# Normalising the first group's softmax on two engines, and re-ordering its hand-over to the MLP

## The chip, the cores and the metric

One NeuronCore of a Trainium2 chip runs the whole program. The metric is device time in microseconds (us) of one execution. Single executions of one kernel scatter by some tenths of a microsecond (before: 295.57 to 295.91 in three runs).

Engines: PE is TensorE's matmul, DVE is VectorE, ACT is ScalarE, POOL is GpSimd, SP issues the DMA transfers. An engine "stands" while it is idle; a "hole" is such a stand between two groups of its instructions.

## The reference, cut to what matters

```python
def _attn_ref(q, k, v):                      # q, k, v: (8, 8, 576, 64)
    k_p = k.reshape(B, H, Sp, 8, D).mean(axis=3)         # pooled by 8: Sp = 72
    v_p = v.reshape(B, H, Sp, 8, D).mean(axis=3)
    scores = scale * np.matmul(q, k_p.transpose(0, 1, 3, 2))
    attn = np.exp(scores - max); attn = attn / (attn.sum(-1) + 1e-9)
    return np.matmul(attn, v_p)

def _moe_ref(x, w_in, w_out):                # x: (4608, 512)
    h = x @ w_in                             # 512 -> 2048
    g = gelu_tanh(h)
    return g @ w_out                         # 2048 -> 512
```

## The kernel before

The 4608 rows are worked in nine groups: one for the first 512 rows of each batch and one for the left-over rows. While TensorE does the MLP of one group, the attention of the next is slipped in between its products, at numbered places called hooks. Group 0 has no predecessor, so its attention runs with nothing to hide behind, in four blocks of 128 rows (j = 0 to 3). Its MLP starts as soon as blocks 0 and 1 are done.

```python
def cast_q(g, j0, j1, eng):        # q from fp32 to bf16, two of the four blocks
    copy(eng, st[g]["qb"][:, j0:j1], st[g]["q"][:, :, j0:j1].rearrange(...))

def norm(g, j, eng):               # one block of the softmax, 8 heads x 72
    nc.vector.reduce_sum(out=den, in_=e, axis=AX.X)
    nc.vector.reciprocal(out=r, in_=den)
    eng.tensor_tensor(out=o, in0=e, in1=r (broadcast), op=ALU.mult)
# ... (cut)
    # front of group 0
    norm(0, 0, nc.vector)
    norm(0, 1, nc.vector)
    e_transpose_pe(0, 0, nc.scalar, "mm")
    q_transpose_pe(0, 2, nc.scalar, "mm")
    q_transpose_pe(0, 3, nc.scalar, "mm")
    warm_up(2, "sc")
    e_transpose_pe(0, 1, nc.vector, "mm")
    for j in (2, 3):
        scores(0, j)
    exps(0, 2)
    for x in range(2):
        values_half(0, 0, x, [nc.vector, nc.scalar][x], "mm")
    exps(0, 3)
# ... (cut)
    # group 1 inside the MLP of group 0; the number is the MLP product ahead of which it is issued
    at(hooks, 72, pool, 1, 0, 4)                     # VectorE, needs k of group 1
    at(hooks, 72, dup_k, 1, 0, 4)
    at(hooks, 72, pool, 1, 4, 5)
    at(hooks, 72, dup_k, 1, 4, 5)
    at(hooks, 80, cast_q, 1, 0, 2, nc.gpsimd)        # needs q of group 1
    at(hooks, 80, cast_q, 1, 2, 4, nc.vector)
    at(hooks, 108, k_transpose_pe, 1, 0, 5)
    at(hooks, 108, k_spread, 1, [nc.vector, nc.vector])
    for j in range(4):
        at(hooks, [114, 118, 122, 125][j], q_transpose_pe, 1, j, nc.vector, "sc")
# ... (cut)
    tail_of_attention(hooks, 1, 188)                 # value products of group 1
```

The softmax here doesn't subtract the row's maximum and nothing guards it: scores larger than these inputs give would overflow.

## Time and profile before

| before | value |
|---|---|
| time, median of 3 runs | 295.87 us |
| span of the profiled run | 293.9 us |
| first MLP product of group 0 | 17.84 us |
| first GELU | 19.98 us |
| last k transpose / first q transpose of group 1 | 32.51 / 33.83 us |
| first scores of group 1 | 36.26 us |
| first MLP product of group 1 | 52.38 us |

A line of a timeline reads: start, time from the first to the last instruction of the line, engine, source line, operation, output<-inputs, shapes, number of instructions, and in brackets how long the engine had been idle and what ended that. A line of the chain reads: start, length, and what the kernel's end was waiting for in that time. The views themselves are shown in the prediction. The waits view adds what an engine waited for in sum: ScalarE and VectorE have long waits everywhere; those that PE does not end up waiting for cost nothing, as PE is busy 97% of the span.

### The profile page before, as it was taken

To read this page: it belongs to the slowest core of one execution; us is meant where nothing else is said; L and a number is where in the kernel's file an instruction comes from. 1 tells how busy PE (TensorE), PEld (TensorE's weight loads), DVE (VectorE), ACT (ScalarE), POOL (GpSimd) and SP (SyncE) were. 2 spreads that over 40 slices of the span, in tenths; PEclk is the share of its full clock that TensorE was granted. 3 is DMA by queue.
4 is the path that set the end of the run, shared out by engine and by line. 5 is a ranking of instruction groups with operands and counts; after the bars stand their busy time and mean duration, and the time that the engine had idled before them with its cause. 6 is when DMAs were issued, how large, how long until landed. Compare 5 with 4: busy or idle time off the path is not lost.

```text
span 293.9 us, 4585 instructions
## 1 busy us (share of the span) xinstructions
PE 286.0 (97%) x1741; PEld 142.7 (49%) x1741; DVE 141.1 (48%) x233; ACT 155.4 (53%) x228; POOL 65.1 (22%) x88
## 2 busy tenths in 40 slices
PE   7889999999999999999999999999999999999996
PEld 3568854445444544454445444544444544444444
DVE  5883769075617570747065806481739100920012
ACT  1475584768067716671576257724673367427500
POOL 3594433221402040114002400240024000100000
PEclk9999999999999999999999999999999999999999
DMA  7999998995599369945994599059944900351012
GB/s 242 357 386 348 382 369 191 342 254 166 129 294 280 116 134 270 265 147 132 263 284 149 126 256 299 7 114 248 285 145 103 170 35 2 81 115 38 0 71 71
DMA packets 73301, 56.32 MB, mean 192 GB/s; under 512 B 45888, under 2 KB 55488, under 8 KB 73280
## 3 DMA queue, kind: packets, MB, share of 16 engines
q1 hardware_dynamic: 73136, 55.98, 70.2%
q8 instruction: 13, 0.21, 0.3%
q10 hardware_dynamic: 144, 0.07, 0.1%
q14 instruction: 8, 0.07, 0.1%
HBM read 36.70 MB, written 9.44 MB: 157 GB/s over the span
## 4 chain that ended last, share of the span: by engine, by line
PE 87%; DMA 7%; SPq 3%; ACT 1%; POOL 1%; issue 0%; DVE 0%; POOLq 0%
PE mm L341 41%; PE mm L325 38%; DMA q_sb<-in_q_dram 5%; DMA w_in_s<-in_moe_w_in_dram 3%; PE xo L291 3%; PE sc L214 2%; PE mm L369 1%; SPq L94 1%; SPq L99 1%; SPq L418 1%; ACT xT L79 1%; PE xo L300 1%; POOL q_b L81 1%; PE mm L336 1%; SPq L92 0%; SPq L111 0%
## 5 line engine op out<-in xcount | busy, mean ns | idle before, releaser
L341 PE MATMUL mm<-w_out_b,gT 128*128 128x512 bf16 x560 | 128.8, 379 | 0.0
L325 PE MATMUL mm<-xT,w_in_b 128*128 128x512 bf16 x512 | 112.0, 379 | 0.3 <-ACT xT L79 0.3
L327 ACT ACTIVATE gT<-mm 128x512 bf16<-128x512 f32 x128 | 76.3, 597 | 38.6 <-PE mm L325 38.6
L341 PEld LDWEIGHTS <-gT 128*128 128x128 bf16 x560 | 52.8, 98 | 59.7 <-issue 2.9
L325 PEld LDWEIGHTS <-w_in_b 128*128 128x128 bf16 x512 | 50.1, 98 | 61.0 <-issue 0.8
L81 DVE COPY osb<-mm 128x512 f32<-128x512 f32 (+2 forms) x37 | 24.2, 658 | 57.6 <-PE mm L341 55.3
L79 ACT CAST xT<-xo 128x1024 bf16<-128x1024 f32 (+1 forms) x18 | 16.6, 967 | 56.9 <-PE xo L291 48.2
L154 POOL TENSOR_TENSOR vbd<-kvb,vmask 128x256 bf16<-128x256 bf16 (+2 forms) x40 | 21.2, 553 | 105.9 <-DVE kvb L134 105.7
L236 DVE TENSOR_REDUCE den<-e 128x8 f32<-128x576 f32 x36 | 26.5, 737 | 36.8 <-ACT e L229 36.8
L132 DVE TENSOR_TENSOR kv<-kv 128x1024 f32<-128x1024 f32 (+3 forms) x19 | 21.9, 1154 | 38.2 <-DMA kv<-in_v_dram 33.3
L229 ACT ACTIVATE e<-sc 128x576 f32<-128x576 f32 x36 | 22.5, 649 | 10.2 <-ACT e L229 5.9
L241 DVE TENSOR_TENSOR eb<-e,r 128x576 bf16<-128x576 f32 x26 | 26.0, 998 | 0.9
L81 POOL CAST q_b<-q_sb 128x2048 bf16<-128x2048 f32 (+2 forms) x9 | 17.6, 1950 | 13.9 <-DMA q_sb<-in_q_dram 13.9
L241 POOL TENSOR_TENSOR eb<-e,r 128x576 bf16<-128x576 f32 x6 | 6.9, 1148 | 58.7 <-ACT e L229 31.4
L336 PE MATMUL mm<-xT,w_in_b 128*128 128x256 bf16 x128 | 15.6, 272 | 0.3 <-DVE xT L81 0.3
L214 PEld LDWEIGHTS <-qT 128*128 128x128 bf16 x128 | 9.9, 98 | 7.3 <-issue 0.8
L214 PE MATMUL sc<-kbd,qT 128*128 128x144 bf16 x128 | 13.1, 226 | 0.4 <-ACT qT L79 0.2
L336 PEld LDWEIGHTS <-w_in_b 128*128 128x128 bf16 x128 | 12.2, 98 | 1.9 <-issue 0.5
L338 ACT ACTIVATE gT<-mm 128x512 bf16<-128x512 f32 x16 | 9.4, 597 | 6.5 <-PE mm L336 6.5
L133 DVE TENSOR_TENSOR kv<-kv 128x512 f32<-128x512 f32 (+3 forms) x19 | 12.4, 651 | 0.6
L536 ACT ACT_TABLE_LOAD x8 | 10.3, 1283 | 0.1
L81 POOL CAST w_in_b<-w_in_s 128x512 bf16<-128x512 f32 (+1 forms) x12 | 9.1, 796 | 1.5 <-DMA w_in_s<-in_moe_w_in_dram 1.5
(58 smaller groups left out, 117.9 us busy)
## 6 DMA issues: line engine op xcount, KB each, us to landing
out_dram<-osb SPq DMA_DIRECT2D x31, 256.0 KB, 6.8
kv<-in_k_dram SPq DMA_DIRECT2D x7, 1024.0 KB, 7.3
q_sb<-in_q_dram SPq DMA_DIRECT2D x7, 1024.0 KB, 5.9
kv<-in_v_dram SPq DMA_DIRECT2D x6, 1024.0 KB, 8.9
w_in_s<-in_moe_w_in_dram SPq DMA_DIRECT2D x8, 512.0 KB, 9.1
w_out_s<-in_moe_w_out_dram SPq DMA_DIRECT2D x4, 1024.0 KB, 13.8
kv<-in_v_dram SPq DMA_DIRECT2D x4, 512.0 KB, 10.1
out_dram<-osb SPq DMA_DIRECT2D x9, 128.0 KB, 2.3
```

The costliest lines, as they stand in the source:

```text
L79: eng.copy(out=out, in_=in_)
L81: eng.tensor_copy(out=out, in_=in_)
L132: add(out=t[:, :, 0:4, :], in0=t[:, :, 0:4, :], in1=t[:, :, 4:8, :], op=ALU.add)
L154: eng.tensor_tensor(out=vbd[p0:128, b, n0:n1, :].rearrange("p (c r) (hh d) -> p c (r hh) d", c=max(m, 1), d=D), in0=kvb[p0:128, 4 + c0:4 + ...
L214: nc.tensor.matmul(out=o, lhsT=qT[:, j, pr, :], rhs=kbd[:, g, pr].rearrange("d hh s -> d (hh s)"), start=True, stop=True)
L229: nc.scalar.activation(out=e.rearrange("p (x h) s -> p x (h s)", x=2), in_=sc[:, :, 0:4 * Sp], func=ACT.Exp, scale=1.0 / 64.0)
L236: nc.vector.reduce_sum(out=den, in_=e, axis=AX.X)
L241: eng.tensor_tensor(out=o.rearrange("p (h s) -> p h s", s=Sp), in0=e, in1=r.unsqueeze(2).to_broadcast([128, H, Sp]), op=ALU.mult)
L325: nc.tensor.matmul(out=hp, lhsT=w_in_b[:, ko, fo * 128:(fo + 1) * 128], rhs=st[g]["xT"][:, ko, :], start=(i == 0), stop=(i == KO - 1))
L327: nc.scalar.activation(out=gT[:, fo, :], in_=hp, func=ACT.Gelu_apprx_tanh)
L336: nc.tensor.matmul(out=hp[:, f, :], lhsT=w_in_b[:, ko, (fo + f) * 128:(fo + f + 1) * 128], rhs=st[g]["xT"][:, ko, c0:c0 + 256], start=(ko ...
L341: nc.tensor.matmul(out=o, lhsT=gT[:, fo, r * 128:(r + 1) * 128], rhs=w_out_b[:, fo, :], start=(fo == 0), stop=(fo == FO - 1))
```

## The change

The intent is to start group 0's MLP sooner. Blocks 0 and 1 are multiplied by the reciprocal of their sums on VectorE (5 heads) and ScalarE (3 heads, one instruction each) side by side; the first value products go ahead of the last scores; two warm-up products go; half of the first w_in chunk is cast on VectorE. The copy of block 2's transposed q moves from ScalarE to VectorE. Further down, the two halves of group 1's q cast change engines, the hooks of its four q transposes move one product later, and that of its value products one earlier.

```diff
--- before.py
+++ after.py
@@ -230,10 +230,17 @@
                              func=ACT.Exp, scale=1.0 / 64.0)
         st[g][("e", j)] = e
 
-    def norm(g, j, eng):
+    def sums(g, j):
         e = st[g][("e", j)]
         den = work.tile([128, H], F32, name="den")
         nc.vector.reduce_sum(out=den, in_=e, axis=AX.X)
+        st[g][("den", j)] = den
+
+    def norm(g, j, eng):
+        e = st[g][("e", j)]
+        if ("den", j) not in st[g]:
+            sums(g, j)
+        den = st[g].pop(("den", j))
         r = work.tile([128, H], F32, name="r")
         nc.vector.reciprocal(out=r, in_=den)
         o = eb[:, j, 128 * 5 - W:]
@@ -245,6 +252,18 @@
                               in0=e.rearrange("p (hh pr) s -> p hh pr s", hh=2),
                               in1=r.rearrange("p (hh pr) -> p hh pr", hh=2).unsqueeze(3).to_broadcast([128, 2, HP, Sp]),
                               op=ALU.mult)
+
+    def norm_two(g, j, h0):
+
+        e = st[g][("e", j)]
+        sums(g, j)
+        r = work.tile([128, H], F32, name="r")
+        nc.vector.reciprocal(out=r, in_=st[g].pop(("den", j)))
+        o = eb[:, j, 128 * 5 - W:].rearrange("p (h s) -> p h s", s=Sp)
+        nc.vector.tensor_tensor(out=o[:, 0:h0], in0=e[:, 0:h0], in1=r[:, 0:h0].unsqueeze(2).to_broadcast([128, h0, Sp]),
+                                op=ALU.mult)
+        for h in range(h0, H):
+            nc.scalar.activation(out=o[:, h], in_=e[:, h], func=ACT.Copy, scale=r[:, h:h + 1])
 
     def eT_tile(g):
         st[g]["eT"] = work.tile([128, 4, 5, 128], BF16, name="eT", bufs=1)
@@ -478,28 +497,30 @@
         scores(0, j)
         exps(0, j)
     pool(0, 5, 7)
+    norm_two(0, 0, 5)
     spread_v(0, nc.gpsimd, (0,))
     pool_pe(0, 7, 9, 1, nc.scalar)
     spread_v(0, nc.gpsimd, (1,))
     cast_q(0, 2, 4, nc.gpsimd)
     spread_v(0, nc.gpsimd, (2,))
-    norm(0, 0, nc.vector)
-    norm(0, 1, nc.vector)
+    norm_two(0, 1, 5)
     e_transpose_pe(0, 0, nc.scalar, "mm")
-    q_transpose_pe(0, 2, nc.scalar, "mm")
+    q_transpose_pe(0, 2, nc.vector, "mm")
     q_transpose_pe(0, 3, nc.scalar, "mm")
-    warm_up(2, "sc")
     e_transpose_pe(0, 1, nc.vector, "mm")
-    for j in (2, 3):
-        scores(0, j)
+    cast_w_in(0, 2, nc.vector)
+    scores(0, 2)
     exps(0, 2)
     for x in range(2):
         values_half(0, 0, x, [nc.vector, nc.scalar][x], "mm")
+    scores(0, 3)
+    sums(0, 2)
     exps(0, 3)
     nc.scalar.preload_act_table_set(GELU_SET)
     norm(0, 2, nc.vector)
     norm(0, 3, nc.vector)
-    for c in range(4):
+    cast_w_in(0, 0, nc.gpsimd)
+    for c in range(1, 4):
         cast_w_in(c, 0, nc.gpsimd)
         cast_w_in(c, 2, nc.gpsimd, 0, 256)
         cast_w_in(c, 2, nc.gpsimd, 256, 512)
@@ -548,14 +569,14 @@
     at(hooks, 72, dup_k, 1, 0, 4)
     at(hooks, 72, pool, 1, 4, 5)
     at(hooks, 72, dup_k, 1, 4, 5)
-    at(hooks, 80, cast_q, 1, 0, 2, nc.gpsimd)
-    at(hooks, 80, cast_q, 1, 2, 4, nc.vector)
+    at(hooks, 80, cast_q, 1, 0, 2, nc.vector)
+    at(hooks, 80, cast_q, 1, 2, 4, nc.gpsimd)
     at(hooks, 108, kT_tile, 1, "sc")
     at(hooks, 108, qT_tile, 1)
     at(hooks, 108, k_transpose_pe, 1, 0, 5)
     at(hooks, 108, k_spread, 1, [nc.vector, nc.vector])
     for j in range(4):
-        at(hooks, [114, 118, 122, 125][j], q_transpose_pe, 1, j, nc.vector, "sc")
+        at(hooks, [115, 119, 123, 126][j], q_transpose_pe, 1, j, nc.vector, "sc")
     at(hooks, 110, cast_w_out, 0, 1, nc.gpsimd)
     at(hooks, 110, cast_w_out, 1, 2, nc.gpsimd)
     at(hooks, 110, cast_w_out, 2, 4, nc.gpsimd)
@@ -575,7 +596,7 @@
     at(hooks, 156, q_tile, 2)
     at(hooks, 156, load_q, 2, 0, 4, nc.sync)
     at(hooks, 156, load_kv, 2)
-    tail_of_attention(hooks, 1, 188)
+    tail_of_attention(hooks, 1, 187)
     mlp_first(0, hooks)
 
     for n_, g in enumerate(seq):
```

## The prediction

> **What bounds the kernel now.** I read the page first: engine shares, then the chain that ended last.
>
> ```profile
> PE 286.0 (97%) x1741; PEld 142.7 (49%) x1741; DVE 141.1 (48%) x233; ACT 155.4 (53%) x228; POOL 65.1 (22%) x88
> ...
> PE 87%; DMA 7%; SPq 3%; ACT 1%; POOL 1%; issue 0%; DVE 0%; POOLq 0%
> ```
>
> TensorE is busy 97% of the 293.9 us span and holds 87% of the chain. Whatever is to be won lies in the 13% that is not PE, and the change touches only the first group, so I asked where that 13% sits: the chain in order of time (start, length, what).
>
> ```profile
> 7.42 8.31 DMA w_in_s<-in_moe_w_in_dram
> 15.75 2.37 SPq L94
> 18.80 13.24 DMA q_sb<-in_q_dram
> 32.19 1.59 POOL q_b L81
> 37.57 2.37 PE mm L341 x11
> 40.20 0.86 PE mm L341 x4
> ```
>
> This is the view that decides the prediction. Until 33.8 us the chain does not run through the softmax of group 0 at all. It runs through the loads: the weights, the issue of group 1's k, group 1's q (landing at about 32 us), then a 1.59 us cast of it on GpSimd. Only then is TensorE the bound. The windows view agrees: DMA share 1.05 to 1.08 in every 10 us stretch from 10 to 40 us, so those landings move with bandwidth and not with the computation.
>
> Then the PE timeline (start, busy, instructions, idle before and its releaser).
>
> ```profile
> 15.43 0.45 PE L255 MATMUL tp<-identb,eb 128*128 128x128 bf16 x5
> 15.72 0.66 PE L214 MATMUL sc<-kbd,qT 128*128 128x144 bf16 x8
> 16.46 1.03 PE L270 MATMUL xo<-eT,vbd 128*128 128x256 bf16 x8
> 17.84 2.02 PE L336 MATMUL mm<-xT,w_in_b 128*128 128x256 bf16 x16 [0.35 <-DVE xT L81]
> ...
> 32.20 0.52 PE L180 MATMUL kT<-identb,kvb 128*128 128x128 bf16 x5
> 32.65 0.83 PE L336 MATMUL mm<-xT,w_in_b 128*128 128x256 bf16 x6
> 33.83 0.40 PE L199 MATMUL tp<-identb,q_b 128*128 128x128 bf16 x4 [0.35 <-POOL q_b L81]
> ```
>
> The first MLP product starts at 17.84. At 32.20 PE transposes group 1's k, and at 33.83 its q, after a hole.
>
> The VectorE timeline shows what the k transposes need.
>
> ```profile
> 28.47 1.23 DVE L132 TENSOR_TENSOR kv<-kv 128x1024 f32<-128x1024 f32 x1 [4.11 <-DMA kv<-in_k_dram]
> ...
> 32.09 0.18 DVE L147 COPY kvb<-kvb 128x64 bf16<-128x64 bf16 x1
> 32.18 0.69 DVE L81 CAST q_b<-q_sb 128x1024 bf16<-128x1024 f32 x1
> ```
>
> Pooling starts the moment k lands (28.47) and its last piece is ready at 32.27, so TensorE arrives at the k transposes with almost no slack.
>
> **What the Trainium skill says.** (1) "SBUF — State Buffer", Who interferes with whom: VectorE and GpSimd share a port pair, taken as an exclusive lock by VectorE casts in a 2-port mode, and contended by two-input VectorE operations. The trace agrees: when both casts of q start at 32.18, VectorE's takes its 0.69 us and GpSimd's 1.58 (1.12 for the same shape at 13.06); a 128x576 multiply takes 0.76 us at 40.08 with GpSimd mostly idle, but 1.01 to 1.15 in the first 22 us. (2) "VectorE: DVE Perf Modes", The TRN2 errata: an fp32 two-input operation takes (N+151)/0.96 ns. For 576 that is 757 ns; the trace has 757. For 360 it gives 532 ns. (3) "ScalarE: Activation LUTs", What ACT_TABLE_LOAD costs: 186 + 0.833 N ns, 93 more for a per-partition operand, 93 of overlap back to back. For N=576 that is 666; the trace has 649. For 72 with a scale operand it gives an estimate of 339 ns, so three take 339 + 2x246 = 0.83 us; no instruction of this form is in the trace before.
>
> **The change, part by part.**
>
> Normalising on two engines. Block 0's multiply now ends near 13.1 (before 13.29), but PE is busy with the v pooling products until 13.34: nothing gained. Block 1: its sum starts about 0.2 earlier, its reciprocal is done near 13.97, VectorE's 5 heads need 0.53 plus a short wait for GpSimd's cast of q, so about 14.65; ScalarE's three end near 14.85. Before, block 1 was ready at 15.37: 0.5 us gained. The price: six ScalarE instructions (2 x 0.83 = 1.7 us), which push the copy of the first transposed block from 13.83-14.52 to about 14.8-15.5.
>
> Transposes and warm-up. Two removed dummy products were 0.43 us in a wait. The second block's transposes go from 15.43 to about 14.9, their VectorE copy from 15.92-16.41 to about 15.4-15.9, so the value products start near 15.95 instead of 16.46. Moving the last scores behind them saves PE nothing in itself: the eight scores (0.66) already fitted into the wait for that copy.
>
> The w_in cast on VectorE. It takes 0.69 us alone (128x1024 fp32, same row as q's cast), but stands in VectorE's order before the copy of the first value product. Its data land at 15.73, and GpSimd's own cast of the other half (1.03 us) starts near 15.5. By the lock, VectorE waits until about 16.45, ends near 17.1, copies xT until 17.75, and the first MLP product starts near 17.75: only 0.1 gained. Unblocked it would be near 17.3. I take 17.75 (17.3 to 17.9).
>
> From there to 24 us. ScalarE has xT's other half, exp and table load about 0.5 earlier: first GELU near 19.45 (before 19.98). The third and fourth blocks' transposes wait on VectorE, which I place 0.2 and 0.4 earlier (19.93 to 19.75, 21.99 to 21.55); the second pair of value products near 22.6 (before 23.03). Gain at 24 us: 0.4 (0.1 to 0.8).
>
> At the k transposes most of that is taken back. PE would come to them at 31.8; the last of the five needs VectorE's copy that ends at 32.27 and hangs on the load. Traced singly, it ran at 32.51 before; it can run at 32.32. So 0.19 of the front's gain survives, whether the front gave 0.2 or 0.8.
>
> The swapped q casts. Traced singly, the six MLP products after the k transposes are issued by 33.31 and PE stands until 33.83 for GpSimd's half, which ended at 33.77 and held the first two blocks. Now VectorE casts those, done at 32.87 in the trace; the first q transposes come after seven products, near 33.2. GpSimd's half (33.77) is needed near 34.5. So the hole of 0.52 goes. This part is worth more than the headline.
>
> Sum: 0.19 + 0.52 = 0.7 us. From there the order hangs on PE: last GELU 36.46 to 35.8, exp, normalisation and spread of v move along, the values of group 1 from 50.30 to 49.6. Putting them one product earlier gains little: their last operands wait for GpSimd's spread, which ended at 50.32 just as PE needed it. The remaining groups are untouched. 295.87 - 0.7 = 295.17.
>
> **The rivals.** (a) The front counts in full: if k's load moved along, 0.4 to 0.8 plus 0.52 would give 294.6 to 295.0. For it: VectorE waits for k only by 4.11 us idle, so earlier data would be used. Against: the queue is saturated, and k's issue waited for a weight landing (14.36), not for an engine. (b) The lock goes the other way at 32.18. The two casts started 6 ns apart. If GpSimd takes the port first, VectorE's half ends near 33.9, the hole stays and the gain is 0 to 0.2: 295.7 to 295.9. For it: 6 ns. Against: VectorE won in the trace, and nothing ahead of it on either engine changes. I give it a quarter. (c) The VectorE cast, twice held by GpSimd, delays the first products past 17.84; the loss would have to exceed the 0.4 slack at the k transposes to show. One in ten. (d) w_out's landing (34.71, cast to 35.38) takes the wait's place: the first output product would come near 35.8, so it just fits.
>
> **Range and chances.** The middle case 295.17, drawn up by (b), gives 295.25. The range 294.75 to 295.8 holds the middle case with 0.2 to 0.3 of run noise (three runs before: 295.57 to 295.91), most of (a), and part of (b). Two per cent is 5.9 us, a third of the whole time before the first MLP product; nothing changed in the other 240 us, so within 2% is as good as certain.
>
> **What would show it.** Right: first MLP product between 17.3 and 17.9; the w_in cast on VectorE well above 0.69 us; the last k transpose still waiting for VectorE near 32.3 with PE idle before it (a new wait of about 0.5); the first q transposes near 33.2 without a hole; the chain running through group 1's k or q load up to 32 us. Wrong: k landing clearly before 28.4; a q cast on VectorE of over 1 us; a PE wait for w_out; any shift between the start of group 2 and the end.

## The result, and the profile after

The changed kernel ran at 295.04 us (median of 4, 294.80 to 295.49), the kernel before at 295.72 (median of 4, 295.51 to 295.91). Ratios and intervals here and below are from fast runs alone; plain means of the same runs give ratios within 0.0005 of them (0.15 us). Here it is 0.9979, 95% interval 0.9962 to 0.9996. That is 0.6 us, or 0.2%.

The PE timeline after, same columns, answers to the lines of before.

```profile
17.68 1.91 PE L355 MATMUL mm<-xT,w_in_b 128*128 128x256 bf16 x16 [0.46 <-DVE xT L81]
...
31.39 0.40 PE L180 MATMUL kT<-identb,kvb 128*128 128x128 bf16 x4
32.52 0.20 PE L180 MATMUL kT<-identb,kvb 64*128 64x64 bf16 x1 [0.74 <-DVE kvb L147]
32.66 0.94 PE L355 MATMUL mm<-xT,w_in_b 128*128 128x256 bf16 x7
33.43 0.39 PE L199 MATMUL tp<-identb,q_b 128*128 128x128 bf16 x4
```

The first MLP product comes only 0.16 us earlier. PE then gains until it reaches the k transposes at 31.39, 0.81 ahead of before. It does four of the five and stands 0.74 us for VectorE's last piece of pooled k. So the fifth runs at 32.52, where it ran before. What is new after that is that the q transposes follow the MLP products without a hole.

VectorE's timeline after shows both ends of this.

```profile
15.87 1.17 DVE L81 CAST w_in_b<-w_in_s 128x1024 bf16<-128x1024 f32 x1
16.96 0.68 DVE L81 CAST xT<-xo 128x512 bf16<-128x512 f32 x1
...
28.66 1.23 DVE L132 TENSOR_TENSOR kv<-kv 128x1024 f32<-128x1024 f32 x1 [5.23 <-DMA kv<-in_k_dram]
...
32.28 0.18 DVE L147 COPY kvb<-kvb 128x64 bf16<-128x64 bf16 x1
32.50 0.69 DVE L81 CAST q_b<-q_sb 128x1024 bf16<-128x1024 f32 x1
```

GpSimd's timeline has this at the same time:

```profile
15.45 1.03 POOL L81 CAST w_in_b<-w_in_s 128x1024 bf16<-128x1024 f32 x1
```

The w_in cast took 1.17 us where a cast of that size takes 0.69. This fits the lock of the prediction: GpSimd's own cast (15.45 to 16.48) held the port pair that the two engines share. The copy of xT, which the first MLP product needs, queued behind it. And VectorE was idle for 5.23 us until k landed.

The chain after is still one of loads up to 28.66, then of VectorE's pooling.

```profile
14.58 14.06 DMA kv<-in_k_dram
28.66 1.24 DVE kv L132
32.72 0.87 PE mm L355 x7
```

k landed 0.2 us later in this profile than in that of before (28.66 against 28.47). This is one source of scatter between runs, so the next table counts from the landing. It is not the only one. PE sometimes also stood for the spread k of a later group: the profile of before lost 0.27 us so in its fifth group (30.11 us instead of 29.84), the profile of after nothing. So the spans of two single profiles (293.9 and 293.1) are not a measure of the change.

### The profile page after: what moved, and what is told of

Its sections match the earlier page's. It is cut to its first block, busy times and chain, and to the rows that moved or that the text cites. A ratio compares the mean times of both kernels' runs of the same rounds, so it can differ in the third digit from the quotient of the medians.

```text
span 293.1 us, 4588 instructions
## 1 busy us (share of the span) xinstructions
PE 286.0 (98%) x1739; PEld 143.5 (49%) x1739; DVE 141.0 (48%) x235; ACT 156.5 (53%) x233; POOL 64.3 (22%) x86
## 4 chain that ended last, share of the span: by engine, by line
PE 87%; DMA 8%; DVE 1%; SPq 1%; ACT 1%; POOL 0%; issue 0%
PE mm L360 41%; PE mm L344 38%; DMA kv<-in_k_dram 5%; DMA q_sb<-in_q_dram 3%; PE xo L310 3%; PE sc L214 2%; PE mm L388 1%; PE mm L355 1%; SPq L99 1%; ACT xT L79 1%; PE xo L319 1%; DVE kv L132 1%; PE tp L199 0%; POOL q_b L81 0%; PE sc L221 0%; DVE kv L133 0%
## 5 line engine op out<-in xcount | busy, mean ns | idle before, releaser
L248 DVE TENSOR_TENSOR eb<-e,r 128x576 bf16<-128x576 f32 x24 | 22.6, 943 | 1.0 <-DVE r L245 0.2
```

What stands on the lines that cost most here:

```text
L248: eng.tensor_tensor(out=o.rearrange("p (h s) -> p h s", s=Sp), in0=e, in1=r.unsqueeze(2).to_broadcast([128, H, Sp]), op=ALU.mult)
```

## The experiments

Twelve runs were made. **Theory:** the 0.6 us come from the exchange of the two q casts; the new front of group 0 is absorbed by the wait for group 1's k. **Rival:** the new front carries the gain.

In the table, "K" is the start of VectorE's pooling of group 1's k, which begins when k has landed. "Scores" and "MLP 1" are the first scores and the first MLP product of group 1, counted from K in the profiled run. "2nd group" is the time from MLP 1's first GELU to that of the group after it (29.84 us in most groups). "Gain" is (1 - ratio) x 295.75. Rows between two rules ran in one call on one chip (chips 7, 7, 6 and 2; that of the first two rows is not on record). The kernel before had medians of 295.70, 295.75, 295.81 and 296.02. K is read from the trace; between two profiles of one kernel, "MLP 1 - K" differs by up to 0.13.

| kernel | time, us (median) | ratio to before (95%) | gain, us | K | scores - K | MLP 1 - K | 2nd group |
|---|---|---|---|---|---|---|---|
| before | 295.72 | 1 | 0 | 28.47 | 7.79 | 23.91 | 29.85 |
| after | 295.04 | 0.9979 (0.9962-0.9996) | 0.62 | 28.66 | 7.08 | 23.33 | 29.84 |
| --- | | | | | | | |
| swap_only | 295.13 | 0.9979 (0.9967-0.9992) | 0.62 | 28.77 | 7.08 | 23.21 | 30.06 |
| front_only | 295.70 | 0.9996 (0.9982-1.0010) | 0.12 | 28.58 | 7.86 | 23.98 | 29.84 |
| late_k | 294.89 | 0.9969 (0.9957-0.9982) | 0.92 | 28.92 | 6.47 | 23.25 | 29.84 |
| w_in_back | 294.77 | 0.9964 (0.9952-0.9977) | 1.06 | 28.45 | 7.08 | 23.20 | 30.13 |
| --- | | | | | | | |
| after_again | 295.33 | 0.9976 (0.9962-0.9990) | 0.71 | 28.56 | 7.08 | 23.20 | 30.10 |
| w_in_back_again | 294.99 | 0.9968 (0.9955-0.9980) | 0.95 | 28.67 | 7.08 | 23.32 | 30.10 |
| late_w_split | 294.83 | 0.9971 (0.9957-0.9984) | 0.86 | 28.72 | 6.47 | 23.24 | 30.18 |
| old_front_split | 295.37 | 0.9988 (0.9974-1.0003) | 0.35 | 28.72 | 7.17 | 23.29 | 30.21 |
| --- | | | | | | | |
| cut_casts | 295.19 | 0.9970 (0.9956-0.9984) | 0.89 | 28.99 | 6.46 | 22.49 | 30.93 |
| cut_casts_late_sc | 294.80 | 0.9953 (0.9940-0.9967) | 1.39 | 28.78 | 6.46 | 22.49 | 30.23 |
| q_second | 295.75 | 0.9991 (0.9975-1.0008) | 0.27 | 28.71 | 7.83 | 23.93 | 29.84 |
| --- | | | | | | | |
| later_sc | 294.23 | 0.9945 (0.9931-0.9958) | 1.63 | 28.40 | 6.48 | 22.51 | 29.84 |

### swap_only: the exchange of the q casts alone

```diff
--- before
-    at(hooks, 80, cast_q, 1, 0, 2, nc.gpsimd)
-    at(hooks, 80, cast_q, 1, 2, 4, nc.vector)
+    at(hooks, 80, cast_q, 1, 0, 2, nc.vector)
+    at(hooks, 80, cast_q, 1, 2, 4, nc.gpsimd)
```

> Before, with only the two casts of group 1's q exchanged between VectorE and GpSimd. Theory (what counts is the hole ahead of group 1's q transposes; the new front of group 0 is absorbed by the wait for group 1's k): 0.5 us faster than before, 295.2 to 295.3, first q transposes about 33.3 to 33.4 instead of 33.83, first MLP product still at 17.8. Rival (the new front carries the gain): under 0.2 us faster.

Its PE timeline:

```profile
17.90 2.02 PE L336 MATMUL mm<-xT,w_in_b 128*128 128x256 bf16 x16 [0.35 <-DVE xT L81]
...
32.27 0.56 PE L180 MATMUL kT<-identb,kvb 128*128 128x128 bf16 x5
32.77 0.83 PE L336 MATMUL mm<-xT,w_in_b 128*128 128x256 bf16 x6
33.43 0.39 PE L199 MATMUL tp<-identb,q_b 128*128 128x128 bf16 x4
```

GpSimd's half of q, which is now the later one, still ends at 34.09:

```profile
32.55 1.54 POOL L81 CAST q_b<-q_sb 128x1024 bf16<-128x1024 f32 x1 [6.18 <-DMA q_sb<-in_q_dram]
```

Two exchanged words give the whole gain of the change: 0.9979, and scores 7.08 us after K, to the hundredth as in the changed kernel, although the first MLP product came at 17.90. The theory holds for the exchange; how close the old front came to costing something here is told below.

### front_only: the change without the exchange

```diff
--- after
-    at(hooks, 80, cast_q, 1, 0, 2, nc.vector)
-    at(hooks, 80, cast_q, 1, 2, 4, nc.gpsimd)
+    at(hooks, 80, cast_q, 1, 0, 2, nc.gpsimd)
+    at(hooks, 80, cast_q, 1, 2, 4, nc.vector)
...                                    # hooks 114, 118, 122, 125 and 188 as before
```

> After, with the q casts and the hooks of group 1 put back as before; the new front of group 0 stays. Theory: 0 to 0.2 us faster than before; PE reaches the k transposes near 31.4 and stands 0.7 us for the last of them, q transposes at 33.8 again. Rival: 0.5 us or more faster, as the changed kernel is.

Its PE timeline:

```profile
31.31 0.40 PE L180 MATMUL kT<-identb,kvb 128*128 128x128 bf16 x4
32.44 0.20 PE L180 MATMUL kT<-identb,kvb 64*128 64x64 bf16 x1 [0.74 <-DVE kvb L147]
32.58 0.83 PE L355 MATMUL mm<-xT,w_in_b 128*128 128x256 bf16 x6
34.00 0.40 PE L199 MATMUL tp<-identb,q_b 128*128 128x128 bf16 x4 [0.59 <-POOL q_b L81]
```

The new front brings PE to the k transposes 0.89 us sooner, PE stands 0.74 for k and then 0.59 for GpSimd's half of q. The ratio of 0.9996 cannot be told from 1, and 7.86 us after K is no better than before's 7.79. The part that gave the change its name is worth nothing that can be measured here.

### q_second: the exchange, but with GpSimd's cast ahead

```diff
--- after
-    at(hooks, 80, cast_q, 1, 0, 2, nc.vector)
     at(hooks, 108, k_spread, 1, [nc.vector, nc.vector])
+    at(hooks, 108, cast_q, 1, 0, 2, nc.vector)
```

> The changed kernel with VectorE's q cast put behind its two copies of the spread k, so that GpSimd takes the shared port first. Theory (the exchange wins because the half that is needed first is cast first): VectorE's cast waits for GpSimd's and ends near 34.2, the first q transposes come at 34.2 to 34.4 instead of 33.43, and the kernel is no faster than before or up to 0.5 us slower. Rival (any order will do, as PE has slack): within 0.2 us of the changed kernel.

GpSimd's timeline, then PE's:

```profile
32.54 1.04 POOL L81 CAST q_b<-q_sb 128x1024 bf16<-128x1024 f32 x1 [5.99 <-DMA q_sb<-in_q_dram]
```

```profile
34.22 0.40 PE L199 MATMUL tp<-identb,q_b 128*128 128x128 bf16 x4 [0.57 <-DVE q_b L81]
```

With the port to itself GpSimd's cast took 1.04 us instead of 1.54, VectorE's half was ready at 34.17, the hole is back, and so is the time (0.9991, scores at K + 7.83). VectorE's cast did not have to wait here, as I had written; it was merely issued at 33.47. So this run does not test who wins the port when both casts are issued together. What it shows is that the half needed first has to be ready first, which the 0.69 us of VectorE's cast made possible.

### w_in_back and w_in_back_again: the w_in cast back on GpSimd

```diff
--- after
-    cast_w_in(0, 2, nc.vector)
...
-    cast_w_in(0, 0, nc.gpsimd)
-    for c in range(1, 4):
+    for c in range(4):
```

> After, with the cast of the second half of the first w_in chunk back on GpSimd. Theory of the port lock: the copy of the first value product no longer queues behind a VectorE cast that took 1.17 us, so the first MLP product comes at 17.2 to 17.3 instead of 17.68. Theory of the absorbed front: the total stays that of the changed kernel within 0.2 us all the same, with a longer stand at the k transposes. Rival to both: the cast on VectorE was needed, the first products wait for GpSimd's later cast, and the total is 0.2 us or more slower.

Its PE timeline:

```profile
17.23 2.02 PE L355 MATMUL mm<-xT,w_in_b 128*128 128x256 bf16 x16
...
32.31 0.20 PE L180 MATMUL kT<-identb,kvb 64*128 64x64 bf16 x1 [0.74 <-DVE kvb L147]
```

The first MLP product comes at 17.23 instead of 17.68: the VectorE cast did cost the front 0.45 us, as expected from the lock. After the k transposes nothing is left of it: scores at K + 7.08 again. But the timed runs were 0.3 us below those of the changed kernel of another call, so both were run in one call:

> The changed kernel once more, as the control of this call: 0.5 to 0.7 us faster than before, 295.0 to 295.2.

> The version with the w_in cast back on GpSimd once more. In its trace, counted from the landing of group 1's k (28.43), the first scores of group 1 come 7.10 us later; in the changed kernel 7.11, in the exchange alone 7.11. Theory (the front is absorbed and the 0.3 us between the two in the timed runs came from when the loads landed): within 0.2 us of the changed kernel in this call. Rival (the VectorE cast costs time after all, by a way the trace does not show): again 0.25 us or more faster than the changed kernel.

Again 0.9968 against 0.9976, 0.24 us (0.34 by the medians), with intervals that overlap by more than that. The theory had said within 0.2 and the rival 0.25 or more, so the theory's bound was missed, if narrowly. In the profiles the two do not differ up to MLP 1 (23.20 and 23.32 against 23.33 and 23.20 after K). The profile of after_again also lost 0.26 in its second group and 0.53 in its fifth, which the first profile of the same kernel did not. Whether w_in_back is better by some 0.2 to 0.3 us stays open; no step in a trace shows it.

### late_k: the k transposes seven products later

```diff
--- after
-    at(hooks, 108, k_transpose_pe, ...)        # and kT_tile, qT_tile, k_spread
+    at(hooks, 115, k_transpose_pe, ...)
-    [115, 119, 123, 126]                       # q transposes
+    [121, 123, 125, 127]
```

> After, with group 1's k transposes seven MLP products later (115 for 108) and the q transposes at 121, 123, 125, 127. Theory (PE stands 0.7 us only because the k transposes are placed before the load can have arrived): 0.2 to 0.7 us faster than the changed kernel; the upper end if nothing else holds, the lower end if the first output products then wait for the cast of w_out, whose data land near 34.7 to 35.1. Rival (PE is bound by its own work, the order does not matter): no change against the changed kernel.

PE's stand for k fell from 0.74 to 0.21 us, and scores come at K + 6.47, 0.62 earlier. By the ratios the kernel is 0.3 us faster than the changed one, the lower part of what was expected, with intervals that overlap. At MLP 1 nothing of it is left; two things took it back. PE's timeline, then VectorE's:

```profile
35.99 0.81 PE L360 MATMUL mm<-w_out_b,gT 128*128 128x512 bf16 x3 [0.19 <-POOL w_out_b L81]
```

```profile
39.08 1.57 DVE L248 TENSOR_TENSOR eb<-e,r 128x576 bf16<-128x576 f32 x1
```

The first output product waits for the cast of w_out, whose data had just landed: the wait that the prediction gave as its last rival. And VectorE's first multiply of group 1 takes 1.57 us instead of 0.76 (0.91 in the changed kernel). MLP 1 starts at K + 23.25; the other kernels so far with exchanged casts have 23.20 to 23.33. I had not seen the second point yet when I planned the next run.

### late_w_split and old_front_split: w_out's first load cut in two, with the new front and the old

```diff
--- late_k, with w_in_back's edit             (old_front_split: the same on swap_only, hook 187)
-            nc.sync.dma_start(out=t, in_=moe_w_out[512 * c:512 * c + 512, :]...)
+        for h in range(2 if c == 0 else 1):
+            n = 2 if c == 0 else 4
+            r0 = 512 * c + 128 * n * h
+            nc.sync.dma_start(out=t[:, n * h:n * h + n, :], in_=moe_w_out[r0:r0 + 128 * n, :]...)
```

> Late k transposes, w_in cast on GpSimd, and the first w_out load cut in two so that its first half lands about 1.3 us earlier. In the run with late k transposes alone the first output product stood from 35.6 to 35.98 for the cast of w_out. Theory (that wait took the place of the k wait): the stand goes or shrinks to under 0.1 us, and the kernel is 0.3 to 0.6 us faster than the changed kernel, 294.5 to 294.8. Rival (GpSimd's cast of q, which ends near 34.2, holds the w_out cast anyway, or the next load takes over): no better than 0.3 us.

> As the run with the cut w_out load, but with the front of group 0 as it was before the change (no shared normalisation, scores ahead of the value products, warm-up in place); the exchanged q casts stay. Theory (the front, worth nothing while the k transposes stand for the load, is worth what is left of its 0.5 to 1.1 us lead once they come later): 0.2 to 0.6 us slower than the version with the new front. Rival (the front is never worth anything, as the loads bound the kernel to 33 us wherever the transposes are): equal within 0.15 us.

The wait for w_out went (first output product 35.44, right behind the scores at 35.20), yet the kernel was at 0.9971, no better than late_k and only 0.15 us better by the ratios than after_again, where 0.3 to 0.6 was expected: a miss. MLP 1 stayed at K + 23.24. Where it went shows on GpSimd, VectorE and PE, in this order:

```profile
37.80 2.03 POOL L81 CAST w_out_b<-w_out_s 128x1024 bf16<-128x1024 f32 x2 [1.65 <-DMA w_out_s<-in_moe_w_out_dram]
```

```profile
38.88 1.55 DVE L248 TENSOR_TENSOR eb<-e,r 128x576 bf16<-128x576 f32 x1
```

```profile
49.62 1.31 PE L310 MATMUL xo<-eT,vbd 32*64 32x512 bf16 x13 [0.20 <-POOL vbd L154]
```

The second w_out load lands and GpSimd casts it in two instructions, the second from about 38.8 to 39.8. VectorE's multiply is issued at 38.88, stands until about 39.7, and the whole of VectorE's row (normalising, then pooling v) and GpSimd's spread of v behind it come as late as ever. PE meets that at the value products of group 1. So a load would set MLP 1 in a roundabout way, through the port pair; the next run tests this.

With the old front, scores come at K + 7.17 instead of 6.47, so the front is worth 0.7 us at that point once the k transposes stand later; at MLP 1 the two are equal (23.29 and 23.24). Their first multiplies of group 1, issued at 39.58 and 38.88, end at 40.48 and 40.44, both behind the same cast of GpSimd. The timed difference of 0.5 us (0.9988 against 0.9971) rests on four runs, one of them at 296.08, and the intervals overlap. I take the expectation as neither met nor refuted in time.

### cut_casts: GpSimd's casts cut in half

```diff
--- late_w_split
-    at(hooks, 110, cast_w_out, 4, 6, nc.gpsimd)
-    at(hooks, 110, cast_w_out, 6, 8, nc.gpsimd)
+    for f in range(4, 8):
+        at(hooks, 110, cast_w_out, f, f + 1, nc.gpsimd)
```

> The run with late k transposes and the cut w_out load, with GpSimd's casts of w_out blocks 4 to 7 as four instructions of 128x512 instead of two of 128x1024. In that run VectorE's first multiply of group 1 took 1.55 us instead of 0.76, and the first MLP product of group 1 came 23.3 us after the landing of group 1's k, as in every kernel with exchanged q casts. Theory (the shared port, held by GpSimd's casts back to back until about 39.7, took the gain back): that multiply takes 0.8 to 1.2 us, and the first MLP product of group 1 comes 22.6 to 23.0 us after k's landing. In the total part of it is lost again where group 2's k is late: 0.1 to 0.4 us faster than the run it is built on. Rival (something else holds the normalisation): 1.5 us and 23.3 again.

VectorE's timeline, then GpSimd's, then PE's:

```profile
39.14 0.76 DVE L248 TENSOR_TENSOR eb<-e,r 128x576 bf16<-128x576 f32 x1
```

```profile
38.09 2.85 POOL L81 CAST w_out_b<-w_out_s 128x512 bf16<-128x512 f32 x4 [1.64 <-DMA w_out_s<-in_moe_w_out_dram]
```

```profile
67.38 0.41 PE L214 MATMUL sc<-kbd,qT 128*128 128x144 bf16 x4 [0.92 <-DVE kbd L81]
```

The multiply takes its 0.76 us, GpSimd's four casts take 2.85 us instead of 2.03 for two, and MLP 1 starts at K + 22.49: 0.75 gained, which shows the long casts of GpSimd to have been the holder. Both are a little better than expected, with some luck: the multiply was issued (39.14) just as a half cast was ending (39.26). The total did not follow (0.9970, where 0.1 to 0.4 us less than late_w_split was expected): a miss. The second group took 30.93 us instead of 29.84: PE stood 0.92 for the spread k of group 2, which comes from its own load and a DMA transpose. The expectation had allowed for a part only.

### cut_casts_late_sc and later_sc: the scores of group 2 later

```diff
--- cut_casts
-                at(hooks, [67, 69, 78, 82][j], scores, n, j)      # and exps
+                s0 = [69, 71, 78, 82][j] if n_ == 1 else [67, 69, 78, 82][j]   # later_sc: 71, 73, 80, 84
+                at(hooks, s0, scores, n, j)
```

> As the run with cut casts, with the first two scores of group 2 two output products later (69 and 71 for 67 and 69, in the second group of the order alone). Theory (a group of 29.84 us takes 30.1 to 30.2 where PE waits for group 2's k, which comes with its load): the second group takes 29.84 again, 0.2 to 0.5 us faster than the run with cut casts, 294.2 to 294.6. Rival (later scores push the softmax and the value products of group 2 late): no gain or slower.

> As the run with cut casts and later scores, with all four scores of group 2 two output products later again (71, 73, 80, 84). Theory (its second group still took 30.23 us, 0.39 over the others, for group 2's k): 29.84 to 29.9 for that group, 0.2 to 0.4 us faster than that run, ratio to before about 0.994 to 0.995. Rival (the softmax and the value products of group 2 come late instead): that group takes 30.2 or more, no gain.

PE's timeline in cut_casts_late_sc, then in later_sc:

```profile
66.91 0.41 PE L214 MATMUL sc<-kbd,qT 128*128 128x144 bf16 x4 [0.23 <-DVE kbd L81]
```

```profile
66.59 0.41 PE L214 MATMUL sc<-kbd,qT 128*128 128x144 bf16 x4
```

The stand shrinks and then goes; the second group takes 30.23 and then 29.84 us. The first of the two had been expected to bring the 29.84 already, and 294.2 to 294.6 us where 294.80 was measured. The ratios follow, 0.9953 and 0.9945, though the intervals of these two, from different chips, overlap (0.9940 to 0.9967 and 0.9931 to 0.9958). later_sc is the best version, 1.6 us under the kernel before and, by the ratios, about 1 us under the changed one (an estimate). It keeps the front of the change, less the w_in cast on VectorE, and its exchanged q casts, and adds the later k transposes, the cut load, the halved casts and the later scores. All kernels gave correct results.

## Why the prediction was right

- **What bounds the first 33 us.** Loads and the q cast behind them, not the softmax: shown by front_only (nothing), swap_only (everything) and by scores at K + 7.08 in the changed kernel, the exchange alone and w_in_back, whose first MLP products lie between 17.17 and 17.90. late_k and old_front_split add that this holds for the place that the k transposes had: later in PE's order, the new front was worth 0.7 us at the scores.
- **The front, step by step.** Block 1 was ready at 15.05, estimated 14.85; ScalarE's three instructions took 0.85, estimated 0.83 from the Trainium skill's "ScalarE: Activation LUTs", What ACT_TABLE_LOAD costs (one instruction: 339 ns estimated, 340 to 357 measured); VectorE's 5 heads of that block took 532 ns, as estimated from "VectorE: DVE Perf Modes", The TRN2 errata, while those of block 0, next to GpSimd's spread of v, took 0.79 us; the first MLP product came at 17.68, estimated 17.75; first GELU 19.46, estimated 19.45. The delay by the lock on the w_in cast, argued from the skill's "SBUF — State Buffer", Who interferes with whom, came as said (1.17 us for 0.69), and w_in_back shows that this cast held the first products back by 0.45 (17.23 without it, estimated 17.3).
- **The one mis-sized term.** The gain at 24 us was put at 0.4 and was 0.9 (second value products at 22.10, not 22.6). I had let VectorE's two multiplies there wait for GpSimd as before. But with one w_in cast fewer, GpSimd now waited for loads at those moments, and both multiplies took 0.76. The missing cast explains a part only: in w_in_back, where GpSimd has it again, they took 1.01 and 0.76. The error cost the forecast nothing, as all of it fell into the stand at the k transposes.
- **What survives at the k transposes, and the hole: 0.19 + 0.52.** Counted from K, scores moved by 0.71, the sum that was predicted. But with the old front, in swap_only, they moved by the same 0.71, so this does not show the 0.19 to be the new front's. k landed 0.30 later in swap_only's profile than in that of before, and PE came to the k transposes only 0.08 later (32.27 against 32.20), so the last of the five waited for VectorE with the old front too, if only by about 0.05. With k landing as early as in the profile of before the new front might be worth the 0.19; no run shows it, and both kernels stand at 0.9979. The hole of 0.52 is shown, the 0.19 is not.
- **The rivals.** (a) k's load did not move with the front; it landed between 28.4 and 29.0 in all profiles, in no order of the fronts. (b) VectorE took the port first in every kernel with its cast placed there (0.69 us, and 1.54 to 1.58 for GpSimd's), so the other outcome stays untested; q_second only shows what a first half that is ready late costs. (c) did not come about: the first products were at 17.68, ahead of 17.84. (d) did not bind in the changed kernel (w_out cast until 35.75, first output product 35.99), but did in late_k.
- **"The remaining groups are untouched."** True of the work, not of the waits: in six of the eight profiles with exchanged casts and uncut w_out casts (q_second left out) the second group lost 0.2 to 0.4 us. In all six its first scores start 0.15 us after VectorE's last copy of the spread k of group 2, as after the stand in cut_casts; in the two without loss they start 0.24 and 0.28 after it. So it is the wait that the last runs deal with. "Any shift between the start of group 2 and the end" had been a sign of being wrong. The first profile of the changed kernel shows none, that of after_again does.
- **The range.** 294.75 to 295.8 also holds the time of the kernel before (295.72), so lying in it says little; what speaks for the mechanism are the marks: q transposes at 33.43 without a hole, the last k transpose after a stand of 0.74 (about 0.5 expected), the w_in cast at 1.17. The weighing of (b) was off: a quarter of 295.8 and three quarters of 295.17 are 295.33, not 295.25.

## What to carry to other kernels

Before a stage is made faster, look in the chain of waits for what the next stage would be waiting for: here the stages up to 23 us got 0.9 us shorter and a load took it back, while exchanging two engine names behind the load gave 0.6 us. When several loads follow each other without slack, a gain must be carried past each of them in turn (here k, w_out, the port pair, then the next group's k), and each step alone shows little or nothing. Small differences are read best as distances from the event that scatters, here the landing of a load, but only where that event is what held the engine: in the profiles of before and old_front_split it did not hold the last k transpose, in the other twelve it did.

## What the Trainium skill lacked or had wrong

- "SBUF — State Buffer", Who interferes with whom, says that the loser blocks until the first instruction finishes. The trace agrees in size, but the loser went on somewhat before the recorded end of the first: the w_in cast issued at 15.87 ended at 17.03, so with 0.69 us of its own work it began near 16.34, 0.14 before the recorded end of GpSimd's cast at 16.48. The same sum gives 0.15 for late_w_split's multiply (1.55 us, 0.76 of its own) and 0.14 for GpSimd's q cast behind VectorE's in before and in swap_only (1.04 of its own). These are estimates, and recorded spans on GpSimd are rough.
- The same section names no remedy of this kind: halving GpSimd's instructions let VectorE's multiply through without a wait (1.55 to 0.76 us, 0.76 and 0.79 in the two later runs), for 0.82 us more of GpSimd's time over four casts in cut_casts.
- No page that I read tells how much the landing of a load behind others in the queue varies from run to run: 0.6 us over these kernels (28.4 to 29.0 us for group 1's k), as much as the whole effect of the change, and 0.1 and 0.2 us between two profiles of one kernel.
